# Mixing layers with operands made seven items ahead, four blocks begun up front, next-layer work in the hidden products, and splits ordered behind the last bank read

## The chip, the cores and the metric

The kernel runs on one core of one Trainium2 chip, as one program. The metric is the device time of one execution in microseconds (us). The kernel before took 1653.02 us, the median of three runs from 1652.94 to 1653.12.

## The reference, cut to what matters

```python
def mix(x):                                   # layers 0 and 2; x is 2048 x 512
    z = layernorm(x)
    a, b = z @ hid_re.T, z @ hid_im.T         # hid: 512 x 512
    return x + seq_re @ a - seq_im @ b        # seq: 2048 x 2048
def geglu(x):                                 # layers 1 and 3
    z = layernorm(x)
    return x + (gelu(z @ w_gate) * (z @ w_up)) @ w_down   # 512 x 1792, 1792 x 512
out = geglu(mix(geglu(mix(x))))
```

All data are float32, and the normalisation has no learned factors.

## The kernel before, in words

**Numbers.** Each float32 operand is split into a high part, which ScalarE writes rounded to fp32r (`split`, L137), and a low part, the rest, which VectorE subtracts (L139). A product is three matmuls, high·high, high·low and low·high (`mm3`, L172 to L174). Whoever wants an operand needs both engines, ScalarE first. `split_minus` (L155, L156) does the same with a changed sign, `split_side` puts both parts of a 256-wide half into one tile.

**Order of a mixing layer.** The product with the sequence matrices comes first, then the one with the hidden matrices. The output's 2048 rows are four blocks b of 512. For each block, the two sequence matrices (re and im) form the two halves of a product that is split 2 by 2 in a scheme with seven products in place of eight: A11·B11, A12·B21, S2·T2, S1·T1, S3·T3, S4·B22 and A22·T4, where S and T are sums of quarters. In the code these are stages of eight items per product: A11, A12, S2 (with S1 and S3, 24 items), S4 (with A22, 16 items). One item is six matmuls: three for each of two PSUM banks (`six`). The block then multiplies its result with the hidden matrices, in groups of twelve matmuls onto four banks (`hid_groups`, L664): EARLY_HID (two groups), MID_HID (four) and LATE_HID (two), and adds x (`x_add`, L212). `plan` (L374) writes down the order. The first FORE blocks have A11 and A12 done ahead of everything; their results but the first's are put away in DRAM on POOL's queue (`put_away`) and fetched again on SP's (`fetched`, L232), and their a11 operands are loaded a second time for S2. A block that isn't among them keeps its a11 tiles and its two banks. In the last block EARLY_HID stood behind S4.

**Operands.** `items` lists all operands of the program in the order of use. `load_next` (L261, its DMA on SP's queue is L270) loads up to RAW = 4 items ahead of the one that is split next, `split_next` makes an operand: for S2 three sums on VectorE and a split. `take` makes operands up to AHEAD items ahead of the one that is used now. Every operand lies in one of 94 tiles of 128 x 512 floats, the slots, given out from a list of free ones, first in first out. A load into a slot waits for the last reader of what lay in it. Besides, four tiles each of two larger buffers ("z" and "x", named wide and xwide in the trace) are lent as slots for a time and reclaimed.

**Rows.** z is normalised by 128 rows: eight first rows and eight second rows. The second rows' norms (`norm_terms`, L494 to L499 on ScalarE, and L516) of layer 2 wait for the x rows that layer 1 ends with. `second_parts` splits one into high and low over 512 columns, used as B21 (columns 0 to 255, by A12) and B22 (256 to 511, by S4). The slots of both came free after S4 of the last block.

**Work beside it.** `step` (L459), called once per item, takes one task from a list `queue`, and every ninth time one from `slow`. In a mixing layer these tasks prepare the next layer: eight norms with turned tiles (`block_steps`, L579; the transposes are L596), put in DRAM and fetched turned (L610); splits of the turned rows; and in layer 0 the first up-weights (`weight_steps`: `load`, sums, four `divide`). They were put on the list at the start of S2 and S4 of the last two blocks.

**Layer 1 and 3** do the up-products, then a down-product whose first part is also a scheme of seven products. In layer 3's second half, partial results (`begun`) are written to DRAM in turned form on POOL's queue (L1144) and loaded again on SP's (`begun_load`, L1158) before the last rows are added and written out.

**Order on each engine.** The program text is not the order of execution: when the kernel is built, a list scheduler places each engine's instructions, with a model of when operands will be there, and the order is then fixed. Each engine works through its instructions in that order. `issue_after` puts an instruction behind a named other one in that order.

## Time and profile before

| what | value |
|---|---|
| median of three runs | 1653.02 us |
| profiled execution | 1656.52 us |
| its span (first to last instruction) | 1654.7 us |
| mean granted TensorE clock | 0.994 |
| VectorE busy, ScalarE busy | 1165.6 us (70%), 827.5 us (50%) |
| moved by DMA | 420.47 MB, mean 254 GB/s |

The profile is of one execution, 1.8 us longer than its span, which itself is not the median run. A row of the timeline has start, busy time, engine, line of the kernel, operation, output and inputs by tile name (p a PSUM bank, s a slot, ws the sequence matrices, wh the hidden ones, wc the down-weights), a count where several lie back to back, and in brackets the idle time before it with what ended it. PE is TensorE, DVE VectorE, ACT ScalarE, POOL GpSimd, SP SyncE; SPq is SP's queue of DMA issues. TensorE's instructions overlap: a matmul is listed with 0.39 us, though the next starts earlier, so that starts have to be compared, and counts.

### The profile page before, as it was taken

To read this page: it belongs to the slowest core of one execution; us is meant where nothing else is said; L and a number is where in the kernel's file an instruction comes from. 1 tells how busy PE (TensorE), PEld (TensorE's weight loads), DVE (VectorE), ACT (ScalarE), POOL (GpSimd) and SP (SyncE) were. 2 spreads that over 40 slices of the span, in tenths; PEclk is the share of its full clock that TensorE was granted. 3 is DMA by queue.
4 is the path that set the end of the run, shared out by engine and by line. 5 is a ranking of instruction groups with operands and counts; after the bars stand their busy time and mean duration, and the time that the engine had idled before them with its cause. 6 is when DMAs were issued, how large, how long until landed. Compare 5 with 4: busy or idle time off the path is not lost.

```text
span 1654.7 us, 22781 instructions
## 1 busy us (share of the span) xinstructions
PE 1624.0 (98%) x7066; PEld 1330.4 (80%) x7066; DVE 1165.6 (70%) x1991; ACT 827.5 (50%) x1591; POOL 226.2 (14%) x409
## 2 busy tenths in 40 slices
PE   9999999999999999999999999999999999999998
PEld 6888887878788888887878877878888887888887
DVE  7998867797876655666778868686964555944574
ACT  7654426544766535556584424364535545533360
POOL 3211002012544122220210000010001000010001
PEclk9999999999999999999999999999999999999999
DMA  9768787889977899977757666778599775896455
GB/s 361 262 211 283 235 249 229 295 258 353 328 270 257 270 347 362 344 268 247 221 174 248 208 220 220 251 227 304 159 307 270 257 236 159 294 298 203 141 183 153
DMA packets 250857, 420.47 MB, mean 254 GB/s; under 512 B 28592, under 2 KB 90800, under 8 KB 249712
## 3 DMA queue, kind: packets, MB, share of 16 engines
q1 hardware_dynamic: 226944, 336.43, 64.3%
q0 software_dynamic: 23792, 82.59, 13.6%
q8 instruction: 56, 0.92, 0.2%
q14 instruction: 65, 0.53, 0.1%
HBM read 334.23 MB, written 84.67 MB: 253 GB/s over the span
## 4 chain that ended last, share of the span: by engine, by line
PE 64%; issue 18%; DMA 10%; DVE 4%; ACT 2%; SPq 1%; POOL 1%; DVEq 0%; POOLq 0%; ACTq 0%
PE p L173 21%; PE p L172 21%; PE p L174 21%; DMA s<-x 3%; DVE s L139 2%; DVE s L163 1%; DMA s<-ws 1%; PE p L705 1%; DVE s L160 1%; DMA x<-s 1%; DMA xwide<-ws 1%; DMA s<-t 1%; DMA s<-wh 1%; ACT s L138 1%; DMA s<-begun 1%
## 5 line engine op out<-in xcount | busy, mean ns | idle before, releaser
L173 PE MATMUL p<-s,s 128*128 128x512 f32 x2334 | 911.6, 391 | 10.7 <-DVE s L139 10.5
L174 PE MATMUL p<-s,s 128*128 128x512 f32 x2334 | 902.3, 391 | 0.5 <-DVE s L156 0.5
L172 PE MATMUL p<-s,s 128*128 128x512 f32 x2334 | 881.8, 392 | 11.5 <-ACT s L138 3.8
L138 ACT ACTIVATE s<-s 128x512 fp32r<-128x512 f32 (+1 forms) x712 | 414.5, 615 | 408.4 <-DVE s L160 96.3
L172 PEld LDWEIGHTS p<-s,s 128*128 128x128 f32 x2334 | 440.6, 189 | 108.9 <-ACT s L138 10.3
L139 DVE TENSOR_TENSOR s<-s,s 128x512 fp32r<-128x512 f32 (+1 forms) x712 | 459.6, 672 | 95.8 <-ACT s L138 66.8
L173 PEld LDWEIGHTS p<-s,s 128*128 128x128 f32 x2334 | 440.0, 189 | 107.3 <-DVE s L139 15.7
L174 PEld LDWEIGHTS p<-s,s 128*128 128x128 f32 x2334 | 440.4, 189 | 94.0 <-DVE s L156 1.3
L163 DVE TENSOR_TENSOR s<-s,p 128x512 f32<-128x512 f32 x283 | 190.4, 683 | 180.4 <-PE p L174 93.6
L160 DVE TENSOR_TENSOR s<-s,s 128x512 f32<-128x512 f32 (+1 forms) x278 | 167.2, 614 | 20.4 <-DMA s<-ws 13.2
L167 ACT ACTIVATE s<-p 128x512 f32<-128x512 f32 x215 | 125.5, 591 | 107.1 <-PE p L174 102.4
L892 ACT ACTIVATE s<-s 128x512 f32<-128x512 f32 x104 | 65.2, 629 | 92.0 <-DVE s L163 89.8
L138 ACT ACTIVATE s<-xwide 128x512 fp32r<-128x512 f32 (+1 forms) x117 | 71.6, 621 | 78.7 <-DVE xwide L163 14.6
L139 DVE TENSOR_TENSOR s<-xwide,s 128x512 fp32r<-128x512 f32 (+1 forms) x117 | 78.8, 680 | 12.7 <-ACT s L138 10.4
L497 POOL TENSOR_SCALAR rstd<-rstd 128x1 f32<-128x1 f32 x48 | 15.7, 328 | 373.6 <-ACT s L496 344.9
L254 POOL DMA_DIRECT2D wb<-s x84 | 45.6, 545 | 98.1 <-ACT s L138 71.1
L906 DVE TENSOR_TENSOR s<-s,s 128x512 f32<-128x512 f32 x77 | 53.1, 689 | 1.9
L163 DVE TENSOR_TENSOR s<-s,s 128x512 f32<-128x512 f32 (+1 forms) x51 | 30.8, 603 | 32.4 <-DMA s<-ws 20.0
L516 ACT ACTIVATE s<-s,shift,rstd 128x512 f32<-128x512 f32 x53 | 42.6, 809 | 11.7 <-DVE shift L489 5.7
L216 POOL DMA_DIRECT2D x<-s x39 | 21.5, 551 | 185.8 <-DVE s L163 184.2
L494 ACT ACTIVATE s<-s 128x512 f32<-128x512 f32 x37 | 23.1, 625 | 36.5 <-DMA s<-x 24.3
L596 DVE STREAM_TRANSPOSE wide<-s 128x512 f32<-128x512 f32 x30 | 21.0, 704 | 24.5 <-ACT s L516 24.4
(110 smaller groups left out, 581.6 us busy)
## 6 DMA issues: line engine op xcount, KB each, us to landing
s<-ws SPq DMA_DIRECT2D x341, 256.0 KB, 4.3
s<-wb SPq DMA_DIRECT2D x294, 256.0 KB, 5.3
s<-wc SPq DMA_DIRECT2D x119, 256.0 KB, 4.3
s<-wh SPq DMA_DIRECT2D x116, 256.0 KB, 4.7
wb<-s POOLq DMA_DIRECT2D x98, 256.0 KB, 4.5
xwide<-ws SPq DMA_DIRECT2D x74, 256.0 KB, 3.6
s<-x SPq DMA_DIRECT2D x65, 256.0 KB, 5.2
wc<-s POOLq DMA_DIRECT2D x49, 256.0 KB, 6.0
```

The lines of the kernel that those rows point to most:

```text
L138: nc.scalar.activation(hi, src, AF.Copy)
L139: nc.vector.tensor_tensor(lo, src, f32(hi), op=ALU.subtract)
L160: nc.vector.tensor_tensor(out, a, b, op=ALU.subtract)
L163: nc.vector.tensor_tensor(out, a, b, op=ALU.add)
L167: nc.scalar.activation(v, src, AF.Copy)
L172: nc.tensor.matmul(ps, ah, bh, start=start, stop=False, skip_group_check=True)
L173: nc.tensor.matmul(ps, ah, bl, start=False, stop=False, skip_group_check=True)
L174: nc.tensor.matmul(ps, al, bh, start=False, stop=stop, skip_group_check=True)
L254: nc.gpsimd.dma_start(a, f32(t))
L516: nc.scalar.activation(z, x, AF.Identity, bias=shift, scale=rstd)
L892: nc.scalar.activation(t, g, AF.Gelu_apprx_tanh)
L906: nc.vector.tensor_tensor(t, t, v, op=ALU.mult)
```

## The change

AHEAD goes from 5 to 7, and FORE of layer 2 from 3 to 4, so that both mixing layers have all four blocks' A11 and A12 up front. `second_parts` makes two split sides, "21" and "22"; the former is freed after A12 of the last block. EARLY_HID of the last block stands behind S2 as in the others. The preparation of the next layer leaves the queue of S2 and S4: `chores_at` gives tasks to blocks 1, 2 and 3, and each hidden group runs its share of those left. Only the fetches of turned tiles stay in S2 of block 3, one every fifth step. "z" is reclaimed in S4 of block 0, not in S2 of block 1. `begun_load` of layer 3 goes by POOL's queue. Loads of rows ahead are laid out anew (`block_steps`, `x_ahead`). And once the first stages of a mixing layer are over (`in_order`, true behind the stages up front), and in every `divide`, each split's ScalarE part is ordered behind the last `copied`, and its VectorE part behind the last `plus` from a bank, that precede it in the program's text.

```diff
--- before.py
+++ after.py
@@ -23,7 +23,7 @@
 EPS = 1e-5
 GELU_A = math.sqrt(2.0 / math.pi)
 GELU_C = 0.044715
-AHEAD = 5
+AHEAD = 7
 MORE = 8
 RAW = 4
 WARM = 16
@@ -34,7 +34,7 @@
 SKEW = 2, 1
 NSLOT = 94
 SEVEN = {(1, 1): 5, (3, 0): 7, (3, 1): 5}
-FORE = {0: 4, 2: 3}
+FORE = {0: 4, 2: 4}
 MADE = 5
 LEAD = 3
 NK = NS // 2
@@ -134,9 +134,17 @@
     def f32(ap):
         return ap.bitcast(F32)
 
+    bank_read, in_order = {}, [False]
+    def behind(engine):
+        return tc.issue_after(bank_read[engine].ins) if in_order[0] and engine in bank_read else ExitStack()
     def split(src, hi, lo):
-        nc.scalar.activation(hi, src, AF.Copy)
-        nc.vector.tensor_tensor(lo, src, f32(hi), op=ALU.subtract)
+        with behind("ACT"):
+            nc.scalar.activation(hi, src, AF.Copy)
+        with behind("DVE"):
+            nc.vector.tensor_tensor(lo, src, f32(hi), op=ALU.subtract)
 
     def split_slot(src):
         hi, lo = sb.get(F32R), sb.get(F32R)
@@ -152,19 +160,23 @@
     def split_minus(src):
 
         hi, lo = sb.get(F32R), sb.get(F32R)
-        nc.scalar.activation(hi, src, AF.Copy, scale=-1.0)
-        nc.vector.scalar_tensor_tensor(lo, src, -1.0, f32(hi), op0=ALU.mult, op1=ALU.subtract)
+        with behind("ACT"):
+            nc.scalar.activation(hi, src, AF.Copy, scale=-1.0)
+        with behind("DVE"):
+            nc.vector.scalar_tensor_tensor(lo, src, -1.0, f32(hi), op0=ALU.mult, op1=ALU.subtract)
         return hi, lo
 
     def minus(out, a, b):
         nc.vector.tensor_tensor(out, a, b, op=ALU.subtract)
 
     def plus(out, a, b):
-        nc.vector.tensor_tensor(out, a, b, op=ALU.add)
+        done = nc.vector.tensor_tensor(out, a, b, op=ALU.add)
+        if id(b) in ps8.held:
+            bank_read["DVE"] = done
 
     def copied(src):
         v = sb.get()
-        nc.scalar.activation(v, src, AF.Copy)
+        bank_read["ACT"] = nc.scalar.activation(v, src, AF.Copy)
         return v
 
     def mm3(ps, a, b, start, stop):
@@ -379,8 +391,6 @@
             if b >= fore:
                 steps += [(b, "A11"), (b, "A12")]
             products = [(b, "S2"), (b, EARLY_HID), (b, "S4"), (b, MID_HID), (b, LATE_HID)]
-            if b == NB - 1:
-                products.insert(2, products.pop(1))
             steps += products
         return steps
 
@@ -537,7 +547,8 @@
         zb[k] = normed(layer, NK + k)
 
     def second_parts(k):
-        zparts["2", k] = split_slot(zb[k])
+        for i in range(2):
+            zparts[f"2{i + 1}", k] = split_side(zb[k][:, half[i]])
 
     def second_rows(layer, k):
         if NK + k not in fresh:
@@ -562,11 +573,11 @@
         zparts["T34", k] = split_slot(u)
         sb.put(u)
 
-    WHERE = {"B21": ("2", 0), "B22": ("2", 2), "T1": ("T12", 0), "T2": ("T12", 2), "T3": ("T34", 0), "T4": ("T34", 2)}
+    WHERE = {"T1": ("T12", 0), "T2": ("T12", 2), "T3": ("T34", 0), "T4": ("T34", 2)}
 
     def z_chunk(name, k, c):
-        if name == "B11":
-            p = zparts["11", k]
+        if name[0] == "B":
+            p = zparts[name[1:], k]
             return p[:, c * P:(c + 1) * P], p[:, 256 + c * P:256 + (c + 1) * P]
         where, c0 = WHERE[name]
         cut = slice((c0 + c) * P, (c0 + c + 1) * P)
@@ -585,7 +596,8 @@
 
             def run():
                 r0 = w * 2 * NT
-                for k in range(i if i == 0 else i + 2, min(i + 3, 2 * NT)):
+                end = 2 * NT if w else i // NT * NT + NT
+                for k in range(i if i == 0 or i + NT == end and not w else i + 2, min(i + 3, end)):
                     fresh["mixed", r0 + k] = x_load_mixed(layer, r0 + k)
                 z = normed(layer, r0 + i, True)
                 part, n = divmod(i, NT)
@@ -659,13 +671,30 @@
 
 
     def mix(layer):
-        hid, sums = {}, {}
+        hid, sums, chores, hid_left = {}, {}, [], [0]
+        def chores_at(b):
+            if b == NB - 3:
+                norms, others = block_steps(layer + 1, 0)
+                later.update(norms=norms[NT:], fetches=others[:ND], others=others[ND:])
+                return norms[:NT]
+            if b == NB - 2:
+                weights = [weight_steps(n) for n in range(2)] if layer == 0 else []
+                norms = later.pop("norms")
+                later["others"] += weights[1][1] if weights else []
+                return [run for load, _ in weights for run in (load,)] + norms + (weights[0][1] if weights else [])
+            return later.pop("others") if b == NB - 1 else []
 
         def hid_groups(b, groups):
 
             first, last = b not in hid, groups is LATE_HID
             if first:
                 hid[b] = [ps8.get() for _ in range(NT)]
+                chores.extend(chores_at(b))
+                hid_left[0] = 2 * ND
             if last:
                 xrows = [x_load(layer, b * NT + i) for i in range(NT)]
             for n, g in enumerate(groups):
@@ -675,6 +704,9 @@
                     mm3(hid[b][i], (hi[:, ts], lo[:, ts]), w, first and n == 0, last and n == len(groups) - 1)
                 sb.put(hi, lo, *w)
                 step()
+                for _ in range(-(-len(chores) // hid_left[0]) if chores else 0):
+                    chores.pop(0)()
+                hid_left[0] -= 1
             if last:
                 for i, ps in enumerate(hid.pop(b)):
                     x_add(layer, b * NT + i, xrows[i], ps)
@@ -685,7 +717,7 @@
                 mm3(ps[c], z_chunk(name, k, c), w, start, stop)
             sb.put(*w)
             if done:
-                sb.put(*(zparts.pop((done, k)) if done[0] == "T" or done == "2" else [zparts.pop((done, k))]))
+                sb.put(*(zparts.pop((done, k)) if done[0] == "T" else [zparts.pop((done, k))]))
             step()
 
         def based(b, c, ps):
@@ -717,7 +749,7 @@
             stream["more"] = 0
             side = [ps8.get() for _ in range(2)]
             for k in range(NK):
-                six(side, "B21", k, k == 0, k == NK - 1)
+                six(side, "B21", k, k == 0, k == NK - 1, "21" if b == NB - 1 else None)
             for c in range(2):
                 v = sums[b][c]
                 if b < FORE[layer]:
@@ -733,15 +765,13 @@
                     cs[0, c] = v
             ps8.put(*side)
 
-        chains, sides, us, rest, opening_weights = {}, {}, {}, [], {}
+        chains, sides, us, later = {}, {}, {}, {}
 
         def s2(b):
             last, fore = b == NB - 1, b < FORE[layer]
             if b == 0:
                 lend("z")
                 lend("x")
-            if b == NB - 3:
-                sb.reclaim("z")
             if fore:
                 chains[b] = [ps8.get() for _ in range(2)]
                 if b:
@@ -749,13 +779,8 @@
                     cs.update({(0, c): fetched((layer, b, c, "sum")) for c in range(2)})
             chain, one, three = chains.pop(b), [ps8.get() for _ in range(2)], [ps8.get() for _ in range(2)]
             sides[b] = one, three
-            if b == NB - 2:
-                norms, others = block_steps(layer + 1, 0)
-                queue.extend([run for norm in norms[:NT] for run in (norm, None)])
-                rest.extend((norms[NT:], others))
-            if last and layer == 0:
-                opening_weights.update((n, weight_steps(n)) for n in range(2))
-                queue.extend([opening_weights[0][0], None, opening_weights[1][0], None, *opening_weights[0][1]])
+            if last:
+                queue.extend([run for fetch in later.pop("fetches") for run in (None, None, None, None, fetch)])
             for i, k in skewed(3):
                 if i == 0:
                     six(chain, "T2", k, fore and k == 0, k == NK - 1)
@@ -779,17 +804,13 @@
 
         def s4(b):
             last = b == NB - 1
+            if b == NB - 4:
+                sb.reclaim("z")
             one, three = sides.pop(b)
             u = us.pop(b)
-            if last:
-                queue.extend(rest[1])
-                if layer == 0:
-                    queue.extend(opening_weights[1][1])
-            if b == NB - 2:
-                queue.extend([run for norm in rest[0] for run in (norm, None)])
             for i, k in skewed(2):
                 if i == 0:
-                    six(one, "B22", k, False, k == NK - 1, "2" if last else None)
+                    six(one, "B22", k, False, k == NK - 1, "22" if last else None)
                 else:
                     six(three, "T4", k, False, k == NK - 1, "T34" if last else None)
                 if k < NK - 1:
@@ -811,10 +832,12 @@
                     weight_load(1)
                 while queue:
                     step()
+            in_order[0] = (b, what) not in plan(layer)[:2 * FORE[layer]]
             if what in stages:
                 stages[what](b)
             else:
                 hid_groups(b, what)
+        in_order[0] = False
 
 
 
@@ -845,6 +868,7 @@
 
         def divide(i):
             def run():
+                before, in_order[0] = in_order[0], True
                 to = place[n][:, i * 1024:min((i + 1) * 1024, 7 * 512)]
                 if i < 3:
                     t = split_slot(src[i])
@@ -857,6 +881,7 @@
                 else:
                     sb.put(*t)
                 sb.put(src[i])
+                in_order[0] = before
             return run
 
         return load, [sums] + [divide(i) for i in range(len(pieces))]
@@ -1155,7 +1180,7 @@
         def begun_load(i):
             t = sb.get()
             part, n = divmod(i, NT)
-            nc.sync.dma_start(t, begun[part][n * P:(n + 1) * P])
+            (nc.sync if before_mix else nc.gpsimd).dma_start(t, begun[part][n * P:(n + 1) * P])
             return t
 
         def plain_rows():
@@ -1273,8 +1298,11 @@
         nc.tensor.matmul(ps[:, :P], ident, ident, start=True, stop=True)
     ps8.put(ps)
 
+    loaded = set()
     def x_ahead(i):
-        if i < NS:
+        if i < NS and i not in loaded:
+            loaded.add(i)
             fresh[i] = x_load(0, i)
 
     for i in range(4):
```

## The prediction, made before the changed kernel ran

> **What bounds the kernel now.** I read the page's engine table first, then rows of TensorE's timeline, then its waits, then busy time by windows, and last the engines that end each wait.
>
> ```profile
> span 1654.7 us, 22781 instructions
> PE 1624.0 (98%) x7066; PEld 1330.4 (80%) x7066; DVE 1165.6 (70%) x1991; ACT 827.5 (50%) x1591; POOL 226.2 (14%) x409
> ```
> ```profile
> 1500.11 0.39 PE L174 MATMUL p<-s,s 128*128 128x512 f32 x1
> 1500.34 0.39 PE L173 MATMUL p<-s,s 128*128 128x512 f32 x1
> ```
>
> TensorE is the bound. Fed matmuls start 0.227 us apart (an average of such rows: two show 0.23), though each is listed with 0.39, so "98%" is not the share at full rate. The change alters no matmul. What can be won is the time in which they start further apart than that:
>
> ```profile
> PE p L173 <- DVE s L139: 10.5, 9, 2.7
> PE p L172 <- ACT s L138: 3.8, 4, 1.5
> PE p L172 <- DMA s<-wc: 3.3, 1, 3.3
> ```
> ```profile
> 110.00:165.00 55.00, 55.00 (x244) 45.37 (x243) 48.96 (x81) 27.40 (x48) 8.62 (x16) 1.00 0.78 254
> ```
> ```profile
> 262.00:288.00 26.00, 24.34 (x101) 18.20 (x99) 20.35 (x34) 17.34 (x39) 5.29 (x7) 1.00 0.78 236
> 340.00:350.00 10.00, 7.55 (x27) 5.77 (x26) 8.83 (x17) 5.54 (x11) 2.69 (x5) 0.83 0.97 322
> 365.00:372.00 7.00, 6.49 (x29) 5.07 (x28) 7.00 (x13) 2.98 (x5) 0.00 (x0) 1.00 0.72 195
> 418.00:428.00 10.00, 8.96 (x40) 7.03 (x40) 6.60 (x15) 3.04 (x7) 4.91 (x9) 1.00 1.03 379
> 775.00:790.00 15.00, 11.69 (x45) 9.17 (x44) 10.00 (x18) 12.39 (x24) 0.00 (x0) 0.89 0.88 292
> 860.00:880.00 20.00, 15.82 (x55) 11.84 (x54) 18.77 (x34) 13.78 (x26) 1.15 (x2) 0.83 0.47 150
> 975.00:1000.00 25.00, 22.22 (x88) 16.99 (x86) 16.81 (x28) 5.92 (x12) 2.16 (x4) 0.93 0.72 245
> 1075.00:1095.00 20.00, 17.17 (x67) 12.93 (x66) 15.06 (x25) 13.03 (x31) 4.09 (x7) 0.91 0.76 252
> 1196.00:1206.00 10.00, 8.12 (x37) 6.34 (x35) 8.56 (x15) 5.18 (x9) 0.00 (x0) 1.00 0.80 216
> 1400.00:1410.00 10.00, 8.58 (x38) 6.78 (x37) 8.20 (x14) 6.94 (x13) 0.00 (x0) 1.00 0.87 289
> ```
>
> The columns are length, then busy time and count of PE, PEld, DVE, ACT, POOL, then granted clock, DMA share, GB/s. A fed window counts some that lie half outside: 55/0.227 is 242.3 and 244 are listed, 1.7 too many. So a window loses its length less (count − 1.7) × 0.227. In the order of the rows: **3.5, 4.3, 0.8, 1.3, 5.2, 7.9, 5.4, 5.2, 2.0, 1.8: 37.4 us.** The first three lie in layer 0's S2 and S4 stages, the fourth at layer 1's start, the fifth late in layer 1, the sixth at layer 2's start, three in layer 2's S2 stages (975 is at block 1's), the last in layer 3. The waits named are for splits (L138 ScalarE, L139 VectorE) or for a load.
>
> Part of the loss is a lower clock behind the stall:
>
> ```profile
> 779.57 0.39 PE L174 MATMUL p<-s,s 128*128 128x512 f32 x1
> 783.27 0.59 PE L172 MATMUL p<-s,s 128*128 128x512 f32 x1 [3.31 <-DMA s<-wc]
> 783.66 0.63 PE L173 MATMUL p<-s,s 128*128 128x512 f32 x1
> 784.09 0.63 PE L174 MATMUL p<-s,s 128*128 128x512 f32 x1
> ```
> ```profile
> 869.61 0.79 PE L173 MATMUL p<-s,s 128*128 128x512 f32 x1 [2.73 <-DVE s L139]
> 870.20 0.63 PE L174 MATMUL p<-s,s 128*128 128x512 f32 x1
> ```
>
> After the stall of 3.31 us matmuls come 0.43 apart, and so after the one of 2.73. The Trainium skill ("TensorE: Matmul & The Clock Gate", Part 1: The HAM clock gate) puts the half rate behind an idle window of about 3.4 us. The trace shows it behind 2.73 us already, so here the measurement decides; by the page a remainder of some 2.5 us would cost no more than itself, by the row half as much again.
>
> **What feeds the stalls.** In S2 an operand passes a load (SP), one to three VectorE sums, and a split. Three things cut in:
>
> ```profile
> 979.57 0.33 SPq L270 DMA_DIRECT2D s<-ws  x1
> 980.07 1.34 SPq L232 DMA_DIRECT2D s<-m_sum  x2
> 981.47 1.37 SPq L270 DMA_DIRECT2D s<-ws  x3
> ```
> ```profile
> 986.80 0.69 DVE L163 TENSOR_TENSOR s<-s,s 128x512 f32<-128x512 f32 x1 [5.89 <-DMA s<-ws]
> 988.15 0.68 DVE L139 TENSOR_TENSOR s<-s,s 128x512 fp32r<-128x512 f32 x1
> 988.76 0.68 DVE L160 TENSOR_TENSOR s<-s,s 128x512 f32<-128x512 f32 x1
> ```
> ```profile
> 250.88 0.63 ACT L494 ACTIVATE s<-s 128x512 f32<-128x512 f32 x1 [4.81 <-DMA s<-x]
> ```
> ```profile
> 340.37 0.63 ACT L138 ACTIVATE s<-s 128x512 fp32r<-128x512 f32 x1 [4.08 <-DMA x<-s]
> ```
> ```profile
> 1084.09 1.89 DVE L596 STREAM_TRANSPOSE wide<-s 128x512 f32<-128x512 f32 x3
> ```
>
> First, room: operand loads are issued late (979.6 to 983) because slots are out, and VectorE waits 5.89 us. Second, chores of the next layer (L494, the transposes L596, the weights' splits) stand ahead of splits in strict engine order and themselves wait for transfers: 4.81 and 4.08 us. Third, VectorE has little spare: a full-size operation is issued each 0.60 us (988.15 to 988.76); an S2 stage holds 8 × 4 + 16 operations for operands and 6 bank reads, 54 × 0.60 = 32.4 us, against 144 matmuls × 0.227 = 32.7 us.
>
> **The change part by part.**
>
> *Seven items ahead, room, chores moved* (AHEAD, second_parts in two sides with "21" freed early, reclaim of "z" earlier, FORE, chores into the hid groups). Counted in the two programs' order, the fewest free slots in layer 2's S2 stages go from 12, 8, 6, 18 (blocks 0 to 3) to 26, 22, 22, 24, in layer 0's b2 from 14 to 22, b3 from 11 to 13. The least distance from the place in TensorE's order that frees a load to go, to its first use, goes from 73 to 108 matmuls in layer 2 b1 S2: 35 × 0.227 = 7.9 us earlier, more than the 5.89 us wait. In b2 S2 40 to 103 (14.3 us), b3 S4 50 to 114, layer 0 b2 S2 72 to 103, b3 S2 72 to 80 (1.8 us: there it is the moved weights that count). The chores go to hid groups, 12 matmuls or 2.7 us each, with one full-size pair of operations for operands: eight groups make 21.8 us, VectorE's own 8 × 0.60 = 4.8, room for the four norms and their transposes. S2's VectorE load falls, counted by the new order, to 23 to 26 of 32.7 us, since sums made early have moved out of it. I take the stalls of layer 0 (3.5 + 4.3 + 0.8) and of layer 2's S2 (5.4 + 5.2 + 2.0) as gone: **−21.2**. Bounds: 0 if these stalls are VectorE's rate alone (rival 2), 21.2 if all is room.
>
> *Layer 1.* At its start less weight work is due when the fourth window opens; distance of loads 46 to 34, a loss. I take half of 1.3: **−0.6** (bounds +0.5 and −1.3). At 779 the load that TensorE waited for had 13 matmuls of lead, now 36: 5.2 us earlier against 3.31. But an L526 norm in that stretch waits for a row loaded later; I leave 1 us: **−4.2** (bounds 0, −5.2).
>
> *Layer 2's opening with four blocks up front.*
>
> ```profile
> 835.00:850.00 15.00, 15.00 (x68) 12.43 (x67) 15.00 (x33) 14.94 (x32) 4.13 (x7) 1.00 0.65 209
> 850.00:862.00 12.00, 12.00 (x55) 9.92 (x54) 6.73 (x15) 12.00 (x31) 2.21 (x6) 1.00 0.27 89
> ```
> ```profile
> 865.13 2.95 ACT L138 ACTIVATE s<-s 128x512 fp32r<-128x512 f32 x5
> ```
>
> ScalarE is full (26.94 of 27 us) with norms and splits of the second rows, and A12 waits for the last of them, at about 868. A fourth A11 stage ahead of A12 gives 48 × 0.227 = 10.9 us more. Against it: its eight items' splits, 8 × 0.52 = 4.2 us of ScalarE (865.13 shows five in 2.95 busy, 0.52 to 0.59 apart), and the last rows of layer 1, which now stand behind 30 matmuls of A11, 6.8 us later. So 10.9 us are gained on that deadline and 11.0 used up: the margin is about nothing, and idle gaps on ScalarE come off it, where before A12 was reached well ahead of its operands. The halved sides cost a second ACT and a second DVE instruction in each of eight parts, between nothing and 8 × 0.52 = 4.2 us, nearer the low end since each moves half the elements. I leave 2.5 us of the stall: **−5.4** (bounds 0 and −7.9). The eight extra a11 loads and four pairs put away and fetched lie in windows where DMA share is 0.27 to 0.65 and cost SP 0.46 us each (981.47, three in 1.37); I set them at nothing. Without that cover they are 8 × 0.46 = 3.7 us on SP.
>
> *Splits behind the last bank read.* No trace of before shows this wait. Bounds: below, a read that was held up by splits comes sooner and frees its bank, at most the 1.8 us of the last window and the like; above, rival 3. Queued behind the waiting split on VectorE and ScalarE are later sums, and TensorE waits for those only seven items, 7 × 6 × 0.227 = 9.5 us, later; a pair of reads is 1.2 us. I take 0.
>
> *Tail.* The partial sums of the last layer are loaded on POOL rather than SP:
>
> ```profile
> 1633.11 2.58 POOL L1144 DMA_DIRECT2D begun<-wide  x4 [3.82 <-DVE wide L163]
> ```
> ```profile
> 1645.22 1.77 SPq L1158 DMA_DIRECT2D s<-begun  x4
> ```
> ```profile
> 1648.32 2.68 DVE L163 TENSOR_TENSOR s<-s,p 128x512 f32<-128x512 f32 x4 [3.68 <-DMA s<-begun]
> ```
>
> The first part's loads now precede the second part's writes in one queue, which so come about 3 us later than 1633.11; the last loads follow them. The last adds (until 1651.0) move by −0.5 to +1.5; I take **+0.8**. The Trainium skill ("DMA: Bandwidth & Descriptors", Specifications) gives GpSimd's path a first byte after about 1 us against 0.6 for SP's, which speaks against this edit: by it the estimate would be 0.4 us more. No run here shows it.
>
> *Opening of the program*: row 4 of x is loaded two loads later: **+0.5** (0 to 1). *New waits* of an order that is new everywhere: **+2** (0 to 6, the upper end a second stall like that at 779).
>
> **Sum:** −21.2 − 0.6 − 4.2 − 5.4 + 0.8 + 0.5 + 2 = **−28.1 us.** The last window's 1.8 stays. The profiled execution took 1656.52 us, 1.8 more than its span; the median of the runs is 1653.02, 3.5 less. 1656.5 − 28.1 = 1628.4 on the profile's scale, 1653.0 − 28.1 = **1625** on the median's. With every bound at its good end: 1653 − 37 + 0.5 = 1616.
>
> **The rivals.**
> 1. *ScalarE still bounds layer 2's opening.* For: two windows at 100%. Against: one stage more of cover. The 7.9 us stay and the late rows add 1.5: 1625 + 5.4 + 1.5 = 1632.
> 2. *VectorE's rate, not room.* For: 32.4 of 32.7 us, and 7.00 of 7.00 at 365. Against: VectorE waited 5.89 us for a load in the middle of such a stage. Layer 2's 12.6 us stay and half of 3.5 + 4.3: 1625 + 16.5 = 1641.
> 3. *Slower: the added wait.* A split of the next operand that stands behind a bank read waits until TensorE has closed that bank, and TensorE then waits for the split. A block has six places where banks are read (chain, two sides, two S4 pairs, hid), eight blocks 48. The gain is used up at 28.1/48 = 0.6 us lost at each, which begins when the split comes more than 9.5 us after its old place. At 1 us each: 1625 + 48 = 1673. Against: reads follow their matmuls within 1.2 us, the lead is eight times that.
> 4. *The order hardly changes,* the queues holding splits there already: 1653. Against: the counts of free slots and distances above.
>
> **How the numbers follow.** Forecast 0.52 (1616 to 1630), rival 1 0.15, rival 2 0.15, something between these and before 0.04, rival 4 0.04, rival 3 0.10. Range 1616 to 1646, which leaves out rivals 3 and 4 and a little more. About 0.2%, 3.3 us, can be told from no change: faster 0.86, same 0.04, slower 0.10.
>
> **What would show it.** Right: the windows at layer 2's S2 stages hold 4.4 matmuls per us; no DVE L163 wait near 6 us for ws; no transposes (line 608 there) or norms inside S2; the PE waits' list without wc at 3.3; at layer 2's opening ScalarE full but TensorE idle under 3 us. Rival 1: a wait for L145/L147 before the first A12. Rival 2: DVE 100% where PE waits in S2. Rival 3: waits of PE for splits which themselves waited for a bank read, near each stage's end. A loss in one new place above 6 us, or a clock under 0.9 in a window that had 1.00, would make the prediction wrong.

## The result and the profile after

The change makes the kernel faster by 0.8%: 1641.30 us against 1654.21 us (medians of eleven runs each), a ratio of 0.9924 with a 95% interval of 0.9909 to 0.9939. That is 12.9 us, less than half of the 28.1 us that were forecast. The runs after spread from 1639.45 to 1650.6 us, those before from 1652.4 to 1658.67.

The profiled execution of the changed kernel was the longest of its eleven, 1650.6 us. Its page, then TensorE's waits:

```profile
span 1648.8 us, 22792 instructions
...
PE 1619.5 (98%) x7066; PEld 1328.5 (81%) x7066; DVE 1163.3 (71%) x2009; ACT 822.5 (50%) x1605; POOL 228.1 (14%) x421
```
```profile
PE p L184 <- DVE s L173: 7.7, 7, 2.5
PE p L184 <- ACT s L145: 5.1, 4, 3.5
PE p L184 <- DVE xwide L173: 5.1, 3, 2.4
PE p L185 <- DVE s L147: 3.0, 3, 1.3
```

Before, TensorE waited 10.5 us for the low part of a split (L139). Now it is 3.0 (L147 is the same line), and 12.8 us are waits for L173, `plus`: mostly reads of a PSUM bank, which TensorE needs before it may open that bank again. Before, `plus` was L163, and all but 0.2 us of the waits for it stand in this row:

```profile
PE p L172 <- DVE s L163: 3.2, 3, 1.9
```

The same kernel ran again beside the first experiments. This execution, 1637.5 us long, has these waits:

```profile
PE p L184 <- ACT s L145: 4.5, 4, 2.8
PE p L184 <- DVE s L173: 2.9, 2, 2.4
PE p L184 <- DVE xwide L173: 2.7, 3, 1.6
```

The windows that answer to those of before, of the execution of 1637.5 us (columns as in the prediction):

```profile
262.00:288.00 26.00, 26.00 (x116) 21.52 (x116) 21.06 (x38) 8.80 (x15) 0.00 (x0) 1.00 0.67 212
...
360.00:374.00 14.00, 10.03 (x36) 7.50 (x35) 9.06 (x15) 7.73 (x14) 0.00 (x0) 0.88 0.92 278
418.00:428.00 10.00, 9.68 (x42) 7.36 (x41) 7.55 (x14) 5.27 (x13) 5.55 (x11) 1.00 0.93 328
775.00:790.00 15.00, 15.00 (x68) 12.43 (x67) 11.24 (x21) 12.30 (x25) 0.00 (x0) 1.00 1.03 369
855.00:870.00 15.00, 11.09 (x37) 8.18 (x36) 15.00 (x30) 13.77 (x28) 1.69 (x3) 0.77 0.46 148
975.00:1000.00 25.00, 25.00 (x112) 20.68 (x112) 19.41 (x32) 10.53 (x18) 1.14 (x3) 1.00 0.65 216
1075.00:1095.00 20.00, 20.00 (x90) 16.56 (x89) 18.85 (x32) 10.03 (x18) 2.05 (x4) 1.00 0.74 247
...
1178.00:1198.00 20.00, 19.54 (x87) 15.83 (x86) 17.07 (x29) 9.20 (x16) 0.00 (x0) 1.00 0.72 247
```

With the prediction's reckoning (length less (count − 1.7) × 0.227) the second window loses 6.2 us, the fifth 7.0, the rest 0.9 or less. So the stalls at 262, 779, 975 and 1078 are gone; the one at layer 2's opening stands; in layer 0's last block 4.3 us were lost near 343 before, and 6.2 are lost near 364 now, at a granted clock of 0.88. By the prediction's own signs, a loss above 6 us in one new place, this speaks against it.

To see all places at once, the table adds up over all matmuls behind 70 us by how much the start of the next one lies further off than 0.227 us, for one profiled execution of each kernel. "Block 0" is 90 to 145 us, "blocks 2, 3" 250 to 400. What each kernel changes is said in the next section.

| kernel | ratio to before (95%) | layer 0, block 0 | layer 0, blocks 2, 3 | layer 1 | opening of 2 | rest of 2 | layer 3 |
|---|---|---|---|---|---|---|---|
| before | 1 | 0 | 8.9 | 6.8 | 7.8 | 13.5 | 1.7 |
| changed (1650.6 us) | 0.9924 | 4.0 | 7.3 | 5.4 | 7.2 | 7.0 | 1.4 |
| changed (1637.5 us) | 0.9927 (0.9914–0.9939) | 2.9 | 6.1 | 1.7 | 7.0 | 0.7 | 0.8 |
| no order | 1.0049 (1.0033–1.0066) | 2.4 | 12.2 | 8.9 | 6.7 | 10.0 | 1.8 |
| five ahead, order | 1.0002 (0.9991–1.0014) | 5.3 | 7.7 | 10.0 | 9.9 | 0.9 | 1.7 |
| five ahead, no order | 0.9961 (0.9950–0.9973) | 1.8 | 7.7 | 5.3 | 9.4 | 0 | 2.0 |
| before with order | 0.9998 (0.9984–1.0012) | 0.7 | 3.2 | 7.6 | 8.1 | 9.2 | 0.9 |
| order in mixing stages only | 0.9926 (0.9913–0.9940) | 3.2 | 4.9 | 6.0 | 6.6 | 2.7 | 1.4 |
| fetches on POOL | 0.9940 (0.9927–0.9952) | 4.5 | 6.6 | 1.6 | 6.8 | 0 | 3.0 |
| fetches flat | 0.9882 (0.9866–0.9898) | 2.7 | 0 | 2.8 | 7.9 | 0 | 2.3 |
| fetches in hidden groups | 0.9913 (0.9893–0.9934) | 3.8 | 0 | 7.5 | 7.7 | 0 | 1.3 |
| the same, no order | 0.9955 (0.9938–0.9971) | 3.3 | 3.8 | 10.5 | 6.9 | 6.1 | 1.3 |
| operand sums behind | 0.9954 (0.9941–0.9966) | 0 | 6.4 | 5.8 | 7.9 | 0 | 1.3 |
| all sums behind | 0.9890 (0.9871–0.9909) | 0.4 | 9.2 | 0 | 7.0 | 0 | 0.9 |
| hidden groups and all sums | 0.9846 (0.9826–0.9866) | 1.0 | 0 | 0 | 6.9 | 0 | 0.7 |
| and half the statistics | 0.9835 (0.9814–0.9855) | 1.4 | 0 | 0 | 6.2 | 0 | 2.0 |
| statistics on VectorE | 0.9935 (0.9920–0.9949) | 3.6 | 6.5 | 3.2 | 8.9 | 0 | 1.7 |
| no statistics | 0.9885 (0.9865–0.9905) | 3.4 | 6.9 | 3.6 | 0 | 0 | 2.2 |
| six more, not eight | 0.9958 (0.9944–0.9972) | 4.0 | 8.0 | 2.1 | 11.0 | 2.3 | 1.6 |
| three blocks up front | 0.9938 (0.9924–0.9953) | 2.4 | 8.0 | 4.7 | 7.6 | 0 | 1.7 |

One execution is one sample: the two of the changed kernel differ by 13 us here. The ratios, of four runs or more, carry the verdicts; the columns tell where to look.

### The profile page after: what moved, and what is told of

It is laid out like the page before. It is cut to its first block, busy times and chain, and to the rows that moved or that the text cites. A ratio compares the mean times of both kernels' runs of the same rounds, so it can differ in the third digit from the quotient of the medians.

```text
span 1648.8 us, 22792 instructions
## 1 busy us (share of the span) xinstructions
PE 1619.5 (98%) x7066; PEld 1328.5 (81%) x7066; DVE 1163.3 (71%) x2009; ACT 822.5 (50%) x1605; POOL 228.1 (14%) x421
## 4 chain that ended last, share of the span: by engine, by line
PE 72%; issue 12%; DMA 9%; DVE 3%; ACT 3%; POOL 1%; SPq 1%; POOLq 0%; DVEq 0%; ACTq 0%
PE p L184 24%; PE p L185 24%; PE p L186 24%; DMA s<-ws 3%; ACT s L145 2%; DVE s L147 1%; DVE s L173 1%; DMA begun<-wide 1%; DMA s<-wb 1%; DMA s<-wgu 1%; ACT s L526 0%; DMA s<-wdc 0%; DMA xwide<-x 0%; DMA s<-x 0%; PE p L737 0%
## 5 line engine op out<-in xcount | busy, mean ns | idle before, releaser
L145 ACT ACTIVATE s<-s 128x512 fp32r<-128x512 f32 (+1 forms) x762 | 434.3, 606 | 414.7 <-DVE s L170 159.2
L147 DVE TENSOR_TENSOR s<-s,s 128x512 fp32r<-128x512 f32 (+1 forms) x762 | 476.8, 662 | 68.1 <-ACT s L145 55.3
L173 DVE TENSOR_TENSOR s<-s,p 128x512 f32<-128x512 f32 x287 | 191.7, 682 | 164.6 <-PE p L186 69.3
L170 DVE TENSOR_TENSOR s<-s,s 128x512 f32<-128x512 f32 (+1 forms) x310 | 187.5, 620 | 80.3 <-DMA s<-ws 56.9
L145 ACT ACTIVATE s<-xwide 128x512 fp32r<-128x512 f32 (+1 forms) x96 | 58.5, 616 | 44.1 <-PE p L185 13.5
L173 DVE TENSOR_TENSOR s<-s,s 128x512 f32<-128x512 f32 (+1 forms) x70 | 43.0, 615 | 52.5 <-DMA s<-ws 26.7
L147 DVE TENSOR_TENSOR s<-xwide,s 128x512 fp32r<-128x512 f32 (+1 forms) x96 | 63.7, 676 | 19.7 <-ACT s L145 19.4
L1169 POOL DMA_DIRECT2D begun<-xwide x8 | 5.2, 655 | 216.6 <-DVE xwide L173 216.4
```

Of the source, the lines that this page charges most:

```text
L145: nc.scalar.activation(hi, src, AF.Copy)
L147: nc.vector.tensor_tensor(lo, src, f32(hi), op=ALU.subtract)
L170: nc.vector.tensor_tensor(out, a, b, op=ALU.subtract)
L173: done = nc.vector.tensor_tensor(out, a, b, op=ALU.add)
```

## The experiments

**The changed kernel again, and without the order of splits.** The edit of the second:

```diff
-        return tc.issue_after(bank_read[engine].ins) if in_order[0] and engine in bank_read else ExitStack()
+        return ExitStack()
```

> The changed kernel as it stands, beside the other three: ratio to before 0.9924 (0.991 to 0.994). Its profile tells which of the stalls of the first profile (which was of the longest of eleven executions, 1650.6 us against a median of 1641.3) come each time. Theory A (queues: transfers of the next layer's turned rows ahead of operand loads on SP's queue in the last blocks' S2, ScalarE at layer 2's opening) expects the stalls near 365, 862 and 1180 to 1191 again, 5 to 7 us each; theory B (the new order of splits behind bank reads) expects TensorE's waits for bank reads (L173) in every block; theory C (VectorE's rate) expects VectorE over 95% busy in the windows of the stalls.

> The changed kernel without the order of splits behind bank reads; room, seven ahead, four blocks up front and moved chores stay. Theory A: within 3 us of the changed kernel, ratio 0.9905 to 0.9945, with the stalls near 365, 862 and 1180 to 1191 unchanged. Theory B (the order costs): faster by 5 us or more, ratio 0.989 or less. If the order is what brought the gain, ratio 0.996 or more.

The changed kernel came out at 0.9927 as before. Without the order it is at 1.0049: slower than the kernel before, and 0.0122 × 1652 = 20 us slower than with it. So the order is what brought the gain; theory A (within 3 us) and theory B (faster) are both refuted on this point. In the trace without the order, VectorE's rows before a bank read, and TensorE's row:

```profile
365.41 1.35 DVE L170 TENSOR_TENSOR s<-s,s 128x512 f32<-128x512 f32 x2 [5.49 <-DMA s<-ws]
366.87 0.69 DVE L147 TENSOR_TENSOR s<-s,s 128x512 fp32r<-128x512 f32 x1
367.48 0.69 DVE L170 TENSOR_TENSOR s<-s,s 128x512 f32<-128x512 f32 x1
369.42 0.69 DVE L147 TENSOR_TENSOR s<-s,s 128x512 fp32r<-128x512 f32 x1 [1.26 <-ACT s L145]
370.03 0.69 DVE L170 TENSOR_TENSOR s<-s,s 128x512 f32<-128x512 f32 x1
370.63 0.69 DVE L147 TENSOR_TENSOR s<-xwide,s 128x512 fp32r<-128x512 f32 x1
371.23 1.28 DVE L147 TENSOR_TENSOR s<-s,s 128x512 fp32r<-128x512 f32 x2
372.44 0.68 DVE L173 TENSOR_TENSOR xwide<-s,p 128x512 f32<-128x512 f32 x1
```
```profile
373.17 0.80 PE L184 MATMUL p<-s,s 128*128 128x512 f32 x1 [3.99 <-DVE xwide L173]
```

The bank's read is the last row. Ahead of it stand five low parts (L147) of operands that are for later, and sums (L170) the first of which waits 5.49 us for a load; VectorE goes through them in order, and TensorE waits 3.99 us. With the order, the same place (execution of 1637.5 us):

```profile
364.48 0.69 DVE L170 TENSOR_TENSOR s<-s,s 128x512 f32<-128x512 f32 x1 [1.23 <-DMA s<-ws]
365.08 0.68 DVE L173 TENSOR_TENSOR xwide<-s,p 128x512 f32<-128x512 f32 x1
368.27 0.69 DVE L170 TENSOR_TENSOR s<-s,s 128x512 f32<-128x512 f32 x1 [2.50 <-DMA s<-ws]
368.88 0.68 DVE L173 TENSOR_TENSOR s<-s,p 128x512 f32<-128x512 f32 x1
```

The splits are gone from ahead of the reads. The sums are not: `plus` and `minus` have no order of this kind. Theory A2 was formed from this: what costs is whatever stands, and waits, in front of a bank read.

**Distance and order apart.**

```diff
-AHEAD = 7
+AHEAD = 5
```

> The changed kernel with operands made five ahead, not seven; order, room, chores stay. Theory A2: fewer operands stand ahead of a bank read, so less depends on the order, but loads are issued later by two items (2.7 us): within 5 us of the changed kernel, ratio 0.992 to 0.996. If seven ahead is what brings the gain: 8 us or more slower than it, ratio 0.997 or more.

> Room and moved chores alone: five ahead and no order. Theory A2: faster than the one with seven ahead and no order (1.0049), because fewer operands are in front of the bank reads, ratio 0.995 to 1.000, and TensorE's waits for bank reads (L173, L179) under 8 us against its 15.4. If room is worth nothing without the order whatever the distance: 1.003 or more.

> The kernel before with the order of splits behind bank reads alone. Theory A2: with five ahead and little room few splits stand ahead of bank reads, and 21 us of its stalls are late operands: ratio 0.996 to 1.000. If the order alone carries the gain: 0.994 or less. If the order costs where there is no room: over 1.002.

Without the order, seven ahead is slower than five (1.0049 against 0.9961), as A2 says. With it, five is slower (1.0002 against 0.9927), which was expected at 0.992 to 0.996, a miss. Before with the order alone is unchanged. So the two edits pay only together: at five ahead the order costs 0.0041 × 1652 = 7 us, at seven it brings 20. One place where TensorE stands in the run with five ahead and order is at 100 us, for a high part:

```profile
100.11 0.73 PE L184 MATMUL p<-s,s 128*128 128x512 f32 x2 [1.85 <-ACT s L145]
```
```profile
95.72 1.39 ACT L145 ACTIVATE s<-s 128x512 fp32r<-128x512 f32 x2 [1.33 <-DVE s L170]
99.43 2.71 ACT L145 ACTIVATE s<-s 128x512 fp32r<-128x512 f32 x5 [2.31 <-DMA m_sum<-s]
```

ScalarE stands still for 2.31 us, until a sum put away (m_sum) has left its slot, and then makes five high parts, the first of which TensorE is waiting for. A split that is held back has less distance left at five ahead. But that the order held this one back is not shown: without the order TensorE waits 1.57 us at 100.67, where it waits 1.85 with it and 1.35 once more at 102.19. By the table the two differ most in layer 1 (10.0 against 5.3 without the order) and in block 0 (5.3 against 1.8).

> The changed kernel with the order of splits only in the mixing stages, not in the weights' divisions. From the stalls of the run without any order: 7 us of its 20 lie in layer 1's first half, where only the divisions' order can act, 13 in the mixing layers. If each acts in its place: about 7 us slower than the changed kernel, ratio 0.995 to 0.998. If the mixing layers' order brings all: within 2 us of the changed kernel.

```diff
-                before, in_order[0] = in_order[0], True
+                before, in_order[0] = in_order[0], False
```

0.9926: the order within the mixing layers brings all of it, and the weights' order nothing that can be told. The 7 us that I had put down to layer 1 came from one execution of each kernel, and what is lost there differs by 3.7 us between two executions of one kernel (1.7 and 5.4 for the changed one).

**The fetches of turned rows.** In layer 0's last block the operand loads were late (5.49 us above). SP issued them behind the fetches, here in the execution of 1637.5 us:

```profile
357.55 2.35 SPq L282 DMA_DIRECT2D s<-ws  x5
360.00 4.77 SPq L622 DMA_DIRECT2D s<-t  x8
364.87 6.72 SPq L282 DMA_DIRECT2D s<-ws  x9
```

> The changed kernel with the fetches of turned rows (L622) issued on POOL's queue instead of SP's, so that no operand load stands behind them. Theory A: the stalls near 365 and 1180 to 1191 (7.3 and 7.1 us) go, 8 to 13 us faster than the changed kernel, ratio 0.984 to 0.988. Theories B and C: no change beyond 2 us, since neither VectorE's work nor the order of splits changes. If the transfers' bandwidth and not the queue is the limit: no change or slower.

```diff
-                        nc.sync.dma_start(
+                        nc.gpsimd.dma_start(
```

0.9940, no gain: SP's queue alone was not the limit. Its windows from 345 to 365, and SP's loads there:

```profile
345.00:355.00 10.00, 10.00 (x46) 8.25 (x45) 9.75 (x16) 6.20 (x11) 6.55 (x12) 1.00 1.05 287
355.00:365.00 10.00, 10.00 (x46) 8.29 (x45) 5.33 (x9) 4.38 (x8) 5.79 (x11) 1.00 1.07 267
```
```profile
345.82 29.46 SPq L282 DMA_DIRECT2D s<-ws  x14
```

The DMA share is over 1, and fourteen loads take 29.46 us to issue: now the DMA engines are full, with the fetches beside the loads.

> The changed kernel whose fetches of turned rows take the tile as it lies in DRAM, in one transfer of 256 KB in place of four strided ones: the turning of layer 1's and 3's first half is left out, the bytes are the same. Theory A (the fetches stand in front of the operand loads, on SP's queue and on the DMA engines): the stall near 365 (6 us) shrinks to 2 or less, those of layer 2's block 3 too, 5 to 9 us faster than the changed kernel, ratio 0.987 to 0.990. If bytes alone count: the stall stays, within 2 us.

```diff
-                    for i in range(P // 32):
-                        cols = turned[part][:, (c * 4 + i) * P:(c * 4 + i + 1) * P]
-                        to = v[i * 32:(i + 1) * 32]
-                        nc.sync.dma_start(
-                            to.rearrange("p (j t) -> p j t", t=P), cols.rearrange("(j p) t -> p j t", p=32)
-                        )
+                    cols = turned[part][:, c * 4 * P:(c + 1) * 4 * P]
+                    nc.sync.dma_start(v, cols)
```

0.9882, and the window of the stall is fed:

```profile
360.00:374.00 14.00, 14.00 (x63) 11.59 (x63) 14.00 (x25) 7.23 (x13) 0.00 (x0) 1.00 0.62 203
```

63 matmuls in 14 us where the changed kernel has 36, and 7 us gained with the same bytes. The strided pieces, not the bytes, cost it. The edit also makes one issue out of four, but with all the issues off SP's queue the stall had stayed (6.6 us). Moved out of S2, and nothing left out:

> The changed kernel with the four fetches of turned rows at the head of the last block's hidden groups, behind its S2, in place of every fifth step of S2; nothing is left out. Theory A (the fetches' strided transfers stand before the operand loads; taking a tile as it lies brought 7 us): the stalls near 365 and 1190 go from S2, 4 to 7 us faster than the changed kernel, ratio 0.988 to 0.990. If they only come later, as a wait in S4 or at the start of the next layer: within 2 us.

```diff
-            return later.pop("others") if b == NB - 1 else []
+            return later.pop("fetches") + later.pop("others") if b == NB - 1 else []
...
-            if last:
-                queue.extend([run for fetch in later.pop("fetches") for run in (None, None, None, None, fetch)])
```

0.9913, 2 us better at most: the stall left S2, and 6.4 us came near 526, in layer 1. There VectorE and TensorE show:

```profile
529.32 0.43 DVE L173 TENSOR_TENSOR s<-s,s 128x256 f32<-128x256 f32 x1 [9.34 <-DMA s<-wgu]
529.66 0.75 DVE L170 TENSOR_TENSOR s<-s,s 128x256 f32<-128x256 f32 x2
530.34 0.68 DVE L173 TENSOR_TENSOR s<-s,p 128x512 f32<-128x512 f32 x1
```
```profile
531.07 0.80 PE L184 MATMUL p<-s,s 128*128 128x512 f32 x1 [4.75 <-DVE s L173]
```

A sum of weights waits 9.34 us for its load, two more sums follow, then the bank read for which TensorE waits 4.75 us. It is A2 once more, with a sum in the split's place.

> Room, seven ahead, fetches in the hidden groups, and no order of splits or sums. If late loads behind the fetches made the order needed, as theory A has it: within 4 us of the same with the order (0.9913), ratio 0.990 to 0.994. Theory A2 (splits made ahead stand before bank reads whatever the loads do, so that without the order seven ahead costs): 10 us or more slower than it, ratio 0.997 to 1.003.

0.9955. Without the order, moving the fetches brings 0.0094 × 1653 = 16 us; with it, 2. So most of the order's 20 us covered for loads that the fetches made late; 7 us (0.9955 against 0.9913) it is worth by itself. Neither theory's range was hit.

**Sums behind bank reads too.**

> The changed kernel in which VectorE's operand sums (L170, L173 from slots) too are ordered behind the last bank read that precedes them. Theory A2 (what is won or lost is how soon a bank is read: operands made ahead that wait for loads stand in front of bank reads on VectorE and ScalarE): the stall near 365 (6.1 us, two bank reads each behind a sum that waits for a load) and those near 135 and 520 go, 4 to 8 us faster than the changed kernel, ratio 0.988 to 0.990. If the late loads themselves set those stalls, the sums are as late as before and TensorE waits for a split in place of a bank: within 2 us.

> The changed kernel with operand sums and weight sums ordered behind bank reads as well. With operand sums alone the opening's 2.9 us went, but 4.3 us came near 530, in layer 1's first half, where a weight sum waits for its load in front of a bank read. Theory A2: both go now, ratio 0.989 to 0.992. If the list scheduler only moves the wait elsewhere: 0.993 to 0.997 as with operand sums alone.

```diff
     def minus(out, a, b):
-        nc.vector.tensor_tensor(out, a, b, op=ALU.subtract)
+        with behind("DVE"):
+            nc.vector.tensor_tensor(out, a, b, op=ALU.subtract)
     def plus(out, a, b):
-        done = nc.vector.tensor_tensor(out, a, b, op=ALU.add)
+        with behind("DVE"):
+            done = nc.vector.tensor_tensor(out, a, b, op=ALU.add)
...
+            before, in_order[0] = in_order[0], True
             plus(v["S1"], v["A21"], v["A22"])
...
             minus(v["S4"], v["A12"], v["S2"])
+            in_order[0] = before
```

The first has only the upper part. It is slower than the changed kernel (0.9954): the stall near 365 turned into a wait for splits, whose loads were as late as before, and 4.3 us came near 530 behind a weight sum. The second, with the weights' sums, is at 0.9890: layer 1's stall is gone, the one in layer 0's last blocks stands at 9.2.

> Both of the two before: fetches in the hidden groups, and all sums behind bank reads. If the two act in different places: their gains add up, ratio 0.985 to 0.988. If late loads are behind both: no better than the better one.

0.9846, 1626.42 us (1626.29 to 1627.72) against 1652.57: 1.5% faster than before, 13 us faster than the changed kernel. TensorE's waits in the whole execution have shrunk to these (L1300 lies at the opening of the program):

```profile
PE p L186 <- ACT s L145: 4.9, 2, 3.5
PE p L1300 <- POOL ident masks.py:199: 1.4, 1, 1.4
PE p L187 <- DVE s L147: 0.7, 1, 0.7
PE p L188 <- DMA s<-wb: 0.4, 1, 0.4
```

No wait for a bank read is left (lines are two further on in this kernel).

**Layer 2's opening.**

> The changed kernel with mean and variance of layer 2's second rows taken on VectorE, as layer 0 does it, so that ScalarE has about 8 x 1.6 us less to do around layer 2's opening. Theory A (ScalarE bounds there): the stall near 862 (7.2 us) goes or halves, 4 to 7 us faster than the changed kernel, ratio 0.988 to 0.990. If something else ends that wait (the rows come too late, or VectorE): no change beyond 2 us.

> The changed kernel with 6 further items ahead, not 8, late in layer 1, so that 13 in all are made ahead as before; the last four matmuls of layer 1 then stand ahead of layer 2's first again, not 30 matmuls behind. Theory late rows: the stall at layer 2's opening (7 us) falls to 3 or less, 4 to 6 us faster than the changed kernel, ratio 0.988 to 0.990. Rival (ScalarE's chain of norms and the slots that it holds, whenever the rows come; the version with five ahead had no such rows and lost 9.4 us there): the stall stays at 6 to 10 us, within 2 us of the changed kernel.

> The changed kernel with three of layer 2's blocks begun up front, not four. If the fourth is worth its room: the stall at layer 2's opening grows from 7 to 10 us or more, since A12 then comes 10.9 us sooner, ratio 0.994 to 0.997. Rival (the fourth block's operands wait for slots that the norms hold): the stall falls below 5 us, ratio 0.989 to 0.991.

> The changed kernel without the statistics of layer 2's second rows: they are scaled by a constant instead, so that ScalarE has 12.8 us less to do, and VectorE nothing more. Theory chain (the stall at layer 2's opening comes from the work of ScalarE and VectorE together behind the last rows of layer 1): it falls from 7 to 2 us or less, 5 to 7 us faster, ratio 0.988 to 0.990. Theory slots (the fourth block's operands wait for slots that normalised rows hold until combined, however fast): it stays at 5 us or more, within 2 us of the changed kernel.

> The version with fetches in the hidden groups and all sums behind bank reads (0.9846), and the statistics of every other one of layer 2's second rows on VectorE, the rest on ScalarE. Theory chain (the work of ScalarE and VectorE behind layer 1's last rows; taken off altogether the stall went, taken to VectorE altogether it stayed): the stall at layer 2's opening falls from 7 to 2 to 4 us, ratio 0.981 to 0.983. If the waits between the engines set the chain and not their work: it stays, ratio 0.984 to 0.986.

The edits of the first, third and fourth are one or two lines each (for the second `MORE = 6`):

```diff
-        if layer == 0:
+        if layer == 0 or layer == 2 and i >= NK:
...
-FORE = {0: 4, 2: 4}
+FORE = {0: 4, 2: 3}
...
+        if layer == 2 and i >= NK:
+            return power, power
```

Statistics on VectorE: the stall is 8.9 us, not less. Rows earlier (six more ahead): 11.0, slower by 5 us. Three blocks up front: 7.6. No statistics at all: gone, at 0.9885, 7 us faster. Six more ahead is no clean test of the rows' time, since ScalarE also took the statistics of the last rows later there (from 850.55 us, after 838.98 in the execution of 1637.5). But without statistics the stall went although layer 1's last four tiles of rows were put away from 839.40 us on, after 837.54 in the execution of 1637.5. So slots and late rows are refuted; the chain of the statistics holds it. Taken to VectorE, ScalarE's work is less, but it waits for it:

```profile
853.83 1.52 ACT L526 ACTIVATE s<-s,shift,rstd 128x512 f32<-128x512 f32 x2 [3.45 <-DVE shift L499]
```

3.45 us in which the splits behind this norm on ScalarE stand as well. Half of them on VectorE, in the best kernel, leaves 6.2 of 6.9 us, where 2 to 4 had been expected if their work set the stall, and its ratio can't be told from that kernel's. The stall speaks for the waits between the engines and against the amount of their work; the ratio, 0.9835, lies between the two expectations. Whether a better order of these norms against the splits would remove the rest was not tried.

## Why the prediction was wrong, point by point

The sum was −28.1 us on the scale of the profile. Profiled against profiled (spans 1654.7 and 1635.7) it is −19.0, and by medians −12.3 in those runs: the execution before was 4.4 us longer than the median of 1652.1, this one 2.3 shorter than its own of 1639.8. The stalls were counted in an execution with more of them than most have, and taken off the median's time. Of the 9.1 us by which −19.0 falls short, 5.8 are layer 0's stalls and 4.6 layer 2's opening; the other terms together came out 1.3 better. The steps, by the table's columns, for the execution of 1637.5 us (in the one of 1650.6, layer 1 kept 5.4 and the rest of layer 2 7.0):

- *Layer 2's S2 stages as gone, −12.6.* Right: 13.5 to 0.7. Their loads came early enough with five ahead as well (0 left, no order), and with three blocks up front (0 left), so what acts there is among the room and the moved chores, which were not tried apart. But with seven ahead and no order 10.0 remain.
- *Layer 0's S2 and S4 as gone, −8.6.* Failed: −2.8. The stall near 263 went, the one in the last block stayed, since the fetches, one every fifth step, were set at nothing. In block 3 the count of distances gave only 8 matmuls, and the text put the gain on moved weights. The fetches flat took the stall away (0 left).
- *Layer 1, −0.6 and −4.2.* Right: 1.4 to 0.9, and 5.4 to 0.8 elsewhere.
- *Layer 2's opening, −5.4.* Failed: 7.8 to 7.0. Rival 1 priced this at 7.9 staying, and it stayed, but not through ScalarE's load alone, as the statistics on VectorE show: what holds it is the chain of the statistics, without which 0 are left. The margin of "about nothing" was too good by 4.6 us.
- *Splits behind the last bank read, 0.* Failed, and it is the step whose mechanism was missed, though the shortfall does not come from it: without it the other edits would have made the kernel 8 us slower, with it 12 us faster. The text bounded its gain by 1.8 us, since it looked at the kernel before, where the order alone changed nothing (0.9998). What a wait is worth has to be asked of the kernel with all other edits in.
- *Tail +0.8, opening of the program +0.5.* Right: from the last matmul's start to the end 6.4 us (1629.31 to 1635.7) after 5.9 (1648.80 to 1654.7); and what is lost ahead of 70 us grew from 6.1 to 6.4.
- *New waits +2.* 2.9 in layer 0's block 0.

Rival 2's time, 1641, is the measured one, by accident: its mechanism is refuted. VectorE was busy 9.06 of 14 us at 360 to 374, and layer 2's stalls went. Rival 3 expected the order to cost, and with five ahead it does, 7 us; that this is by its mechanism isn't shown, and with seven ahead the gain outweighs it. Rival 4 is refuted by the run without the order.

## What to carry to other kernels

An engine that works in strict order must not hold a buffer's last read behind an instruction that can wait for a load: working further ahead puts more such instructions there, and may lose more than it hides. Put the reads first for every kind of instruction, sums as well as splits, and change distance and order together, since each alone can cost. And scale a sum of stalls to the median of the runs: 6.7 of the 15.8 us between forecast and result lay in which executions had been profiled.

## What the runs showed of the hardware that was not expected

With strided fetches in pieces of 128 floats among the loads, the DMA engines move less at the same busy share. In the run with fetches on POOL the share was 1.05 and 1.07 at 287 and 267 GB/s (above); 20 us earlier, when the first fetches were only being issued (336.48 us on), these were the rows:

```profile
325.00:335.00 10.00, 10.00 (x46) 8.29 (x45) 10.00 (x18) 3.52 (x6) 4.86 (x10) 1.00 1.02 382
335.00:345.00 10.00, 10.00 (x46) 8.29 (x45) 5.95 (x11) 2.42 (x4) 4.96 (x10) 1.00 1.04 374
```

A full share at some 380 GB/s against some 277. The earlier rows also hold writes to DRAM (x and wb, on POOL's queue), so the same stretch of two kernels is the better comparison, the changed one at 1637.5 us and the one with flat fetches:

```profile
345.00:365.00 20.00, 19.22 (x85) 15.58 (x83) 12.44 (x20) 7.25 (x13) 0.00 (x0) 1.00 0.83 224
```
```profile
345.00:365.00 20.00, 20.00 (x90) 16.57 (x89) 18.22 (x31) 12.48 (x23) 0.00 (x0) 1.00 0.85 297
```

At nearly the same share, 224 GB/s with the strided pieces and 297 without. The Trainium skill ("DMA: Bandwidth & Descriptors", Specifications) puts the least transfer for line rate at 512 bytes, which is just the length of these pieces; here, mixed with the others, they did not reach it.

The half clock followed shorter stalls than the prediction had: in the kernel before one of 1.51 us (and another of 0.18 just behind it), but not one of 1.89:

```profile
990.18 0.47 PE L172 MATMUL p<-s,s 128*128 128x512 f32 x1 [1.51 <-ACT s L138]
...
991.29 0.50 PE L172 MATMUL p<-s,s 128*128 128x512 f32 x1 [0.18 <-DVE wide L163]
...
992.44 0.63 PE L172 MATMUL p<-s,s 128*128 128x512 f32 x1
```
```profile
1201.06 0.50 PE L172 MATMUL p<-s,s 128*128 128x512 f32 x1 [1.89 <-DVE s L163]
```

The window 1196 to 1206 had clock 1.00 in the prediction's rows. So the length of a stall alone doesn't tell whether it costs half as much again.
